# Four of six row transposes moved from TensorE to VectorE's 32 x 32 blocks and 32 small transfers per pass

## The chip, the cores and the metric

The kernel runs on one core of one Trainium2 chip. The metric is the device time of the whole kernel in microseconds; the median of three runs before the change is 877.59 us (877.58 to 877.67). The core has TensorE (matrix products, PE in the profile; its weight loads are PEld), VectorE (DVE), ScalarE (ACT), GpSimd (POOL) and SyncE (SP), each with its own queue of instructions in program order. They meet only through semaphores. Transfers are issued here by SyncE and, after the change, also by ScalarE.

## The reference

Three steps in a row, on 4 sequences of 448 positions with 768 channels (12 heads of 64):

```python
scores = scale * np.matmul(q, k.transpose(0, 1, 3, 2)) - np.log(S)
attn = 1.0 / (1.0 + np.exp(-scores)); x = attn @ v        # attention

xk = mu_k * x + (1 - mu_k) * x_prev; xr = mu_r * x + (1 - mu_r) * x_prev
k = np.maximum(xk @ w_k, 0.0); v = k * k @ w_v            # gated part
x = 1.0 / (1.0 + np.exp(-(xr @ w_r))) * v

h = np.maximum(x.transpose(0, 2, 1) @ w_tok1, 0.0) @ w_tok2   # along the positions
u = x + h.transpose(0, 2, 1)
out = u + np.maximum(u @ w_ch1, 0.0) @ w_ch2              # along the channels
```

The step that matters here is `x.transpose(0, 2, 1)`: the gated rows lie with channels on partitions, and the product with `w_tok1` needs them with positions on partitions.

## The kernel before

All work is done twice, for two sequences each time (`b0` is 0, then 2). The two sequences lie side by side, so that a tile is 128 channels by 2 x 448 = 896 columns, and 768 channels are six such tiles, m = 0 to 5. One pass is `attention`, `first_part`, `second_part`.

Every product is made with operands split into a high and a low part of a rounded format: three matmuls (high x high, high x low, low x high) stand for one. `products` writes them for one weight block: 896 columns are cut into 512 and 384, first all matmuls of one piece, then all of the other; the next call begins with the piece that the last one ended with.

Weights come as raw 64-bit numbers. For each block of weights there is a transfer (`w_raw`, SyncE), two ScalarE passes (`w_form`, L220 and L221), two VectorE passes (`w_join`, L224 and L227), a ScalarE copy to the rounded high part (`w_high`, L265, tile `whi`) and a VectorE subtraction for the low part (`w_low`, L269, tile `wlo`). `weights()` takes the next block and puts the steps for blocks further ahead in the list `due`; `products` runs one of them (`tick`) after every second slice of its loop. While block i is being multiplied, the queues get: high part of i+2; low part of i+2 and form of i+3; nothing; join of i+3 and the raw transfer of i+5. There are two raw buffers, two form buffers and three split buffers.

The stage that the change touches is the third loop of `first_part`: for m = 0 to 5, two weight blocks (`part` 0 and 1) of four slices each make 128 channels of `k*k @ w_v` in PSUM, and L416 multiplies them by the gate in `rows[:, m]`. Below, "the product of m" is that VectorE instruction. `hooks` maps a slice number to a function that is called after that slice in the second piece of a block: for m from 1 on, after slice 0 of part 0, `y_transpose(m - 1)`. It lets TensorE transpose the row tile m - 1 in eight pieces against an identity matrix (L352), and ScalarE and VectorE write high and low part from PSUM into `y` (L354 to L357; the last 64 positions have their low part in the upper 64 partitions).

Then come three pieces of the product with `w_tok1`, each on two row tiles (0 and 1, 2 and 3, 4 and 5), of 22 matmuls of 512 columns each. `y_transpose(NT - 1)` for tile 5 stands after piece 0, so that its eight transposes wait for the product of m = 5. The order of the work is that of the program; nothing is rearranged.

Buffers around the change: `xes`, six tiles with the attention output (two sequences of 1 + 448 columns; the first column is zeroed once at the start, L154), not in use in the stage; `kqs`, three tiles for queries and keys, not in use either; `two`, which holds `y` here.

Of the kernel before, what the change touches and what calls it, by code (L numbers as in the profile page):

```python
# [9 lines left out]
F32 = mybir.dt.float32  # L10
# [4 lines left out]
ALU = mybir.AluOpType  # L15
PSUM = bass.MemoryType.PSUM

B, H, S, D = 4, 12, 448, 64
# [4 lines left out]
P = 128  # L23
NT = C // P
NPAIR = H // 2
TAIL = S - 3 * P
W = 2 * S

WIDE = ((0, 512), (512, W - 512))
WARM = 9  # L30
KQ = 4 * P + S


def f32(ap):
    return ap.bitcast(F32)
# [3 lines left out]
def kernel(  # L39
# [17 lines left out]
    PE, ACT, DVE, POOL, SP = nc.tensor, nc.scalar, nc.vector, nc.gpsimd, nc.sync  # L57
# [4 lines left out]
    const = pool("const", 1)  # L62
# [12 lines left out]
    warm = const.tile([P, 1], F32, tag="warm", name="warm")  # L75
    ident = const.tile([P, P], F32, tag="ident", name="ident")
    mus = {n: [const.tile([P, NT], F32, tag=m + n, name=m + n) for m in ("mu", "om")] for n in "kr"}
    xes = [const.tile([P, 2, 1 + S], F32, tag="xe%d" % i, name="xe") for i in range(NT)]
    const.tile([P, 8], F32, tag="pad", name="pad")
    one = const.tile([P, 2 * NT * W], F32R, tag="one", name="one")  # L80
    two = const.tile([P, 2 * 4 * 2 * C], F32R, tag="two", name="two")
    three = const.tile([P, 4 * W], F32R, tag="three", name="three")
# [21 lines left out]
    def beside(ap):  # L104
        return ap.rearrange("p (b n) -> p b n", b=2)

    kqs = [const.tile([P, KQ], F32, tag="kq%d" % i, name="kq") for i in range(3)]
    vns = [const.tile([P, 7, D], F32, tag="vn%d" % i, name="vn") for i in range(4)]
    more = [const.tile([P, W], F32, tag="more%d" % i, name="more") for i in range(2)]
    kq_high = [two[:, 2 * i * KQ : (2 * i + 1) * KQ] for i in range(2)]  # L110
# [38 lines left out]
    for name, src in (("k", mu_k), ("r", mu_r)):  # L149
        m, om = mus[name]  # L150
        SP.dma_start(out=m, in_=src)
        DVE.tensor_scalar(out=om, in0=m, scalar1=-1.0, scalar2=1.0, op0=ALU.mult, op1=ALU.add)
    for t in xes:
        POOL.memset(t[:, :, 0:1], 0.0)  # L154

    places = [rows[:, m] for m in range(NT)] + more
    att = {}
# [162 lines left out]
    def products(ps, pieces, parts, at=0, count=None, hooks={}, in_turn=False):  # L320
        count = count or len(parts)
        runs = [pieces] if in_turn else [(p,) for p in pieces]
        if runs[-1][-1][1] == last[0]:
            runs.reverse()
        last[0] = runs[-1][-1][1]
        for r, run in enumerate(runs):
            for i, (wh, wl, xh, xl) in enumerate(parts, at):
                passes = [(wh, xh), (wh, xl), (wl, xh)] if xl is not None else [(wh, xh), (wl, xh)]
                for n, (w, x) in enumerate(passes):
                    for a, cols in run:  # L330
                        PE.matmul(  # L331
                            ps[:, a : a + cols],
                            w,
                            x[:, a : a + cols],
                            start=(i == 0 and n == 0),
                            stop=(i == count - 1 and n == len(passes) - 1),
                        )
                if in_turn or len(runs) == 1 or i % 2 or i == at + len(parts) - 1:
                    tick()
                if i in hooks and r == len(runs) - 1:  # L340
                    hooks[i]()
# [4 lines left out]
    def y_transpose(m):  # L346
        ps = new_ps()
        psv = ps.rearrange("p (r b c) -> p r b c", r=4, b=2)
        for r in range(4):
            n = P if r < 3 else TAIL  # L350
            for b in range(2):
                PE.transpose(psv[:n, r, b], rows[:, m, b * S + r * P : b * S + r * P + n], ident)  # L352
        hi, lo = (t[:, :, m] for t in y)
        ACT.copy(hi[:, :3], psv[:, :3])  # L354
        DVE.tensor_tensor(out=lo[:, :3], in0=psv[:, :3], in1=f32(hi[:, :3]), op=ALU.subtract)  # L355
        ACT.copy(hi[:TAIL, 3], psv[:TAIL, 3])
        DVE.tensor_tensor(out=hi[TAIL:, 3], in0=psv[:TAIL, 3], in1=f32(hi[:TAIL, 3]), op=ALU.subtract)  # L357

    def attention(b0):
        for t in range(NT):  # L360
            i, xe = b0 * NPAIR + 2 * t, xes[t]
            if t + 1 < NT:
                load_kq(i + 2)
            scores(i)
            if t + 1 < NT:
                load_kq(i + 3)
                load_v(i + 2)
                load_v(i + 3)
            if b0 == 0 and t == 0:
                w_raw(2)  # L370
            scores(i + 1)
            if t + 1 < NT:
                split_kq(i + 2)
                split_kq(i + 3)
            if b0 == 0 and 1 <= t < 5:
                w_form(t)
                w_join(t)
                w_raw(t + 2)
                w_high(min(t - 1, 3))
                w_low(min(t - 1, 3))  # L380
            ps = [values(i), values(i + 1)]
            value_tails(i, ps[0], xe)
            value_tails(i + 1, ps[1], xe)
            mix("r", t, xr, xe)

    def first_part(b0):
# [11 lines left out]
        for m in range(F // P):  # L398
# [7 lines left out]
            ACT.copy(hi, t)  # L406
            DVE.tensor_tensor(out=lo, in0=t, in1=f32(hi), op=ALU.subtract)

        for m in range(NT):
            ps = new_ps()  # L410
            for part in range(2):
                w = weights()
                parts = [(w[0][:, t], w[1][:, t], *kk(4 * part + t)) for t in range(4)]
                hooks = {0: lambda: y_transpose(m - 1)} if m and part == 0 else {}
                products(ps, WIDE, parts, 4 * part, 8, hooks)
            DVE.tensor_tensor(out=rows[:, m], in0=rows[:, m], in1=ps[:, :W], op=ALU.mult)  # L416

        wt1 = [weights()]
# [155 lines left out]
```

## Time and profile before

| What | Value |
|---|---|
| median of 3 runs | 877.59 us |
| the profiled execution | 878.26 us, its span 876.4 us |
| TensorE matmul busy | 871.5 us, 99% of the span |
| VectorE busy | 542.3 us, 62% |
| ScalarE busy | 416.3 us, 47% |
| chain of work that ended last | 98% TensorE |
| DMA engines, mean busy share | 33% |
| granted TensorE clock | 1.0 in all |

The span is the part of the execution that the profile shows; 1.9 us of the profiled execution lie around it. Busy shares are means over stages. Times in the rows are microseconds from the start of the span unless marked ns. A line such as L352 is a line of the kernel before.

### The profile page before, as it was taken

The page shows a single profiled execution, that of the slowest core. Times are in us where ns is not written, and L with a number is a line of the kernel's source. Part 1 is how long each engine was busy: PE and PEld are TensorE (multiplying, and loading weights), DVE is VectorE, ACT ScalarE, POOL GpSimd, SP SyncE. Part 2 cuts the span into 40 slices and gives each one's busy share as a digit, 9 for nine tenths or more (in the row PEclk, how much of TensorE's full clock was granted, in tenths as well). Part 3 has the DMA queues.
Part 4 walks back from the last instruction along what each step waited for, and adds up shares of the span by engine and source line. Part 5 has one row for each costly group of instructions (what it writes and reads, how often), then busy time and mean ns, then how long its engine had stood idle before and what let it go on. Part 6 is the DMA issues. An engine that isn't in the chain of part 4 may idle for free.

```text
span 876.4 us, 11347 instructions
## 1 busy us (share of the span) xinstructions
PE 871.5 (99%) x4637; PEld 735.2 (84%) x4637; DVE 542.3 (62%) x608; ACT 416.3 (47%) x550; POOL 1.3 (0%) x13
## 2 busy tenths in 40 slices
PE   9999999999999999999999999999999999999998
PEld 4557989899888989898955589899998898989897
DVE  3877976565676555555656498665566755555551
ACT  5894545444444433443366644555444444334420
POOL 0000000000000000000000000000000000000000
PEclk9999999999999999999999999999999999999999
DMA  7452323232322333334664023322234133333321
GB/s 268 142 172 87 124 86 101 86 97 96 132 73 73 109 109 108 108 108 153 235 234 133 22 75 109 105 84 74 95 101 164 37 109 108 109 108 108 109 99 63
DMA packets 29571, 98.90 MB, mean 113 GB/s; under 512 B 3536, under 2 KB 13008, under 8 KB 29520
## 3 DMA queue, kind: packets, MB, share of 16 engines
q1 hardware_dynamic: 29232, 97.73, 33.0%
q8 instruction: 36, 0.59, 0.3%
q10 hardware_dynamic: 288, 0.46, 0.1%
q14 instruction: 15, 0.12, 0.0%
HBM read 92.67 MB, written 5.51 MB: 112 GB/s over the span
## 4 chain that ended last, share of the span: by engine, by line
PE 98%; DVE 1%; DMA 1%; issue 0%; ACT 0%; POOL 0%; SPq 0%; ACTq 0%; POOLq 0%
PE ps L331 82%; PE ps L179 7%; PE ps L193 6%; PE ps L201 1%; PE ps L352 1%; DMA out_dram<-rows 1%; PE ps L141 0%; DVE two L161 0%; DVE rows L480 0%; DVE wd L227 0%; DVE wlo L269 0%; ACT rows L187 0%; DVE wd L224 0%; DVE rows L474 0%; POOL rows L138 0%
## 5 line engine op out<-in xcount | busy, mean ns | idle before, releaser
L331 PE MATMUL ps<-one,whi 128*128 128x512 f32 (+1 forms) x1152 | 323.7, 363 | 0.0
L331 PE MATMUL ps<-two,whi 128*128 128x512 f32 (+1 forms) x1044 | 295.8, 365 | 0.0
L331 PEld LDWEIGHTS ps<-one,whi 128*128 128x128 f32 x1152 | 211.5, 188 | 24.9 <-issue 1.4
L331 PEld LDWEIGHTS ps<-two,whi 128*128 128x128 f32 x1044 | 192.5, 188 | 23.2 <-DVE two L355 0.4
L331 PE MATMUL ps<-one,wlo 128*128 128x512 f32 (+1 forms) x576 | 207.3, 363 | 0.0
L331 PE MATMUL ps<-two,wlo 128*128 128x512 f32 (+1 forms) x528 | 191.1, 366 | 0.0
L265 ACT CAST whi<-wd 128x768 fp32r<-128x768 f32 (+1 forms) x104 | 80.8, 777 | 134.3 <-PE ps L331 91.8
L331 PEld LDWEIGHTS ps<-one,wlo 128*128 128x128 f32 x576 | 107.9, 188 | 11.4
L224 DVE SCALAR_TENSOR_TENSOR wd<-wd,raw 128x768 uint32<-128x768 uint32 (+1 forms) x104 | 92.2, 887 | 33.6 <-ACT raw L221 33.3
L331 PEld LDWEIGHTS ps<-two,wlo 128*128 128x128 f32 x528 | 98.9, 188 | 11.4
L269 DVE TENSOR_TENSOR wlo<-wd,whi 128x768 fp32r<-128x768 f32 (+1 forms) x104 | 91.6, 880 | 9.4 <-ACT whi L265 8.9
L227 DVE SCALAR_TENSOR_TENSOR wd<-raw,wd 128x768 uint32<-128x768 uint32 (+1 forms) x104 | 92.2, 887 | 3.6
L220 ACT ACTIVATE wd<-raw 128x768 f32<-128x768 f32 (+1 forms) x104 | 88.3, 849 | 3.5 <-DMA raw<-in_moe_w_ch_dram 3.5
L221 ACT ACTIVATE raw<-raw 128x768 uint32<-128x768 uint32 (+1 forms) x104 | 86.7, 833 | 0.0
L462 DVE SCALAR_TENSOR_TENSOR one<-ps,one 128x896 fp32r<-128x896 f32 x24 | 26.2, 1092 | 71.1 <-ACT one L461 71.1
L461 ACT ACTIVATE one<-ps 128x896 fp32r<-128x896 f32 x24 | 22.1, 921 | 95.8 <-PE ps L331 95.8
L480 DVE TENSOR_TENSOR rows<-rows,ps 128x896 f32<-128x896 f32 x23 | 25.0, 1088 | 67.4 <-PE ps L331 67.4
L187 ACT ACTIVATE rows<-ps 128x896 f32<-128x896 f32 x72 | 59.8, 938 | 11.5 <-PE ps L179 9.7
L179 PEld LDWEIGHTS ps<-two 64*128 64x128 f32 x528 | 47.8, 184 | 13.2 <-issue 7.4
L179 PE MATMUL ps<-two 64*128 64x448 f32 x528 | 57.7, 370 | 0.0
L193 PE MATMUL ps<-rows,vn 128*64 128x448 f32 x240 | 48.0, 545 | 0.1
L193 PEld LDWEIGHTS ps<-rows,vn 128*64 128x64 f32 x240 | 16.1, 136 | 26.8 <-issue 21.8
(69 smaller groups left out, 564.4 us busy)
## 6 DMA issues: line engine op xcount, KB each, us to landing
raw<-in_moe_w_ch_dram SPq DMA_DIRECT2D x48, 768.0 KB, 4.1
raw<-in_moe_w_k_dram SPq DMA_DIRECT2D x16, 768.0 KB, 4.2
raw<-in_moe_w_v_dram SPq DMA_DIRECT2D x24, 512.0 KB, 3.2
raw<-in_moe_w_r_dram SPq DMA_DIRECT2D x12, 768.0 KB, 4.2
kq<-in_k_dram SPq DMA_DIRECT2D x23, 256.0 KB, 4.5
vn<-in_v_dram SPq DMA_DIRECT2D x24, 224.0 KB, 4.5
kq<-in_q_dram SPq DMA_DIRECT2D x23, 224.0 KB, 4.8
out_dram<-rows SPq DMA_DIRECT2D x23, 224.0 KB, 2.1
```

Of the source, the lines that this page charges most:

```text
L179: PE.matmul(ps[:, h * 512 : h * 512 + S], x[me, at : at + P], y[me], start=(n == 0), stop=(n == len(passes) - 1),)
L187: ACT.activation(a, banks(ps), AF.Sigmoid, bias=-math.log(S), scale=1.0 / math.sqrt(D))
L193: PE.matmul(ps[h * D : h * D + D, :S], vns[i % 4][:, 3 * h + c], att[i % 2, c][:, h], start=(c == 0), stop=False)
L220: ACT.activation(f32(dst), f32(raw[..., 1]), AF.Copy, scale=2.0**-112)
L221: ACT.activation(raw[..., 0], raw[..., 0], AF.Copy, bias=0.4375, scale=0.875 * 2.0**-29)
L224: DVE.scalar_tensor_tensor(out=dst, in0=dst, scalar=3, in1=raw[..., 0], op0=ALU.logical_shift_left, op1=ALU.bitwise_or)
L227: DVE.scalar_tensor_tensor(out=dst, in0=raw[..., 1], scalar=0x80000000, in1=dst, op0=ALU.bitwise_and, op1=ALU.bitwise_or)
L265: ACT.copy(halves[i][0], forms[i])
L269: DVE.tensor_tensor(out=halves[i][1], in0=forms.pop(i), in1=f32(halves[i][0]), op=ALU.subtract)
L331: PE.matmul(ps[:, a : a + cols], w, x[:, a : a + cols], start=(i == 0 and n == 0), stop=(i == count - 1 and n == len(passes) - 1),)
L462: DVE.scalar_tensor_tensor(out=lo, in0=ps[:, :W], scalar=0.0, in1=f32(hi), op0=ALU.max, op1=ALU.subtract)
L480: DVE.tensor_tensor(out=rows[:, m], in0=rows[:, m], in1=ps[:, :W], op=ALU.add)
```

## The change

`y_transpose` stays for the row tiles 4 and 5. For the tiles 0 to 3 (`TURNED = 4`) three new functions replace it.

`y_turn(m)`: two VectorE instructions (one for each sequence) that transpose the tile within blocks of 32 x 32, into a buffer `turned`. There are two such buffers, one for tiles 0 and 1 in the memory of `xes`, one for tiles 2 and 3 in that of `kqs`, so both of these become one tile each that is cut up. A block transposed in place sits on the wrong partitions: `y_carry` moves the blocks to where they belong by 16 transfers for two tiles, issued by ScalarE, 32 in a pass. Each reads 32 partitions x 8 runs x 64 numbers (256 bytes a run, 64 KB in all) and writes 32 partitions of `staged`. `y_split(m)`: for each sequence two ScalarE copies and two VectorE subtractions, now from `staged` in SBUF, eight instructions in place of four.

`between(m, part)` sets the places, as hooks after the slices 0 to 3 of each block: `y_turn(m - 1)` where the transposes were; the transfers two at a time from the third slice of m = 2 and of m = 4 on; `y_split(0)` and `y_split(1)` in part 1 of m = 3, `y_split(2)` and `y_split(3)` in part 1 of m = 5. The zeroed columns of `xes`, which `staged` and `turned` overwrite, are zeroed at the start of each `attention`. One unused tile grows from 8 to 40 numbers.

```diff
+BLK = 32
+TURNED = 4
...
-    xes = [const.tile([P, 2, 1 + S], F32, tag="xe%d" % i, name="xe") for i in range(NT)]
-    const.tile([P, 8], F32, tag="pad", name="pad")
+    xes = const.tile([P, NT * 2 * (1 + S)], F32, tag="xe", name="xe")
+    const.tile([P, 40], F32, tag="pad", name="pad")
+    turned = xes[:, : 16 * P]
+    staged = xes[:, 16 * P : 32 * P].rearrange("p (s b r c) -> p s b r c", s=4, b=2, r=4)
...
-    kqs = [const.tile([P, KQ], F32, tag="kq%d" % i, name="kq") for i in range(3)]
+    kqs = const.tile([P, 3 * KQ], F32, tag="kq", name="kq")
+    turned = [t.rearrange("p (b g c) -> p b g c", b=2, c=2 * BLK) for t in (turned, kqs[:, : 16 * P])]
+    kqs = [kqs[:, i * KQ : (i + 1) * KQ] for i in range(3)]
...
+    def y_turn(m):
+        at = m % 2 * BLK
+        for b in range(2):
+            DVE.transpose(
+                turned[m // 2][:, b, : S // BLK, at : at + BLK],
+                rows[:, m, b * S : (b + 1) * S].rearrange("p (g c) -> p g c", c=BLK),
+            )
+
+    def y_carry(src):
+        def move(d, s):
+            ACT.dma_start(out=staged[d * BLK : (d + 1) * BLK, s], in_=src[s * BLK : (s + 1) * BLK, :, d::4])
+
+        return [lambda d=d, s=s: move(d, s) for d in range(4) for s in range(4)]
+
+    def y_split(m):
+        at = m % 2 * BLK
+        for b in range(2):
+            src = staged[:, :, b, :, at : at + BLK].rearrange("p s r c -> p r s c")
+            hi, lo = (t[:, :, m, b].rearrange("p r (s c) -> p r s c", c=BLK) for t in y)
+            ACT.copy(hi[:, :3], src[:, :3])
+            DVE.tensor_tensor(out=lo[:, :3], in0=src[:, :3], in1=f32(hi[:, :3]), op=ALU.subtract)
+            ACT.copy(hi[:TAIL, 3], src[:TAIL, 3])
+            DVE.tensor_tensor(out=hi[TAIL:, 3], in0=src[:TAIL, 3], in1=f32(hi[:TAIL, 3]), op=ALU.subtract)
...
+            def first():
+                if part == 0 and 0 < m <= TURNED:
+                    y_turn(m - 1)
+                elif part == 0 and m:
+                    y_transpose(m - 1)
+
+            def some():
+                for _ in range(2):
+                    if moves:
+                        moves.pop(0)()
+
+            def third():
+                if part == 0 and m in (2, 4):
+                    moves.extend(y_carry(turned[m // 2 - 1]))
+                some()
+
+            def second():
+                if part == 1 and m in (3, 5):
+                    y_split(m - 3)
+                some()
+
+            def fourth():
+                if part == 1 and m in (3, 5):
+                    assert not moves
+                    y_split(m - 2)
+                some()
+
+            return {at: first, at + 1: second, at + 2: third, at + 3: fourth}
...
-                hooks = {0: lambda: y_transpose(m - 1)} if m and part == 0 else {}
-                products(ps, WIDE, parts, 4 * part, 8, hooks)
+                products(ps, WIDE, parts, 4 * part, 8, between(m, part))
```

Two places in the order of instructions matter below. The first is VectorE's queue in m = 5 of the first pass. Before the change, from the low part of the second `w_tok1` block on (`wd` and `raw` are weight buffers, `rows` the gated tile, L416 the product of m = 5):

```order
L269 TENSOR_TENSOR wlo<-wd,whi 128x512
L224 SCALAR_TENSOR_TENSOR wd<-wd,raw 128x768
L227 SCALAR_TENSOR_TENSOR wd<-raw,wd 128x768
L416 TENSOR_TENSOR rows<-rows,ps 128x896
L269 TENSOR_TENSOR wlo<-wd,whi 128x768
```

The same stretch after the change (`xe` holds `staged`, `two` holds `y`; L387 and L389 are the subtractions of `y_split`, L483 is the product of m = 5):

```order
L276 TENSOR_TENSOR wlo<-wd,whi 128x512
L387 TENSOR_TENSOR two<-xe,two 128x3x128
L389 TENSOR_TENSOR two<-xe,two 64x128
L387 TENSOR_TENSOR two<-xe,two 128x3x128
L389 TENSOR_TENSOR two<-xe,two 64x128
L231 SCALAR_TENSOR_TENSOR wd<-wd,raw 128x768
L234 SCALAR_TENSOR_TENSOR wd<-raw,wd 128x768
L387 TENSOR_TENSOR two<-xe,two 128x3x128
L389 TENSOR_TENSOR two<-xe,two 64x128
L387 TENSOR_TENSOR two<-xe,two 128x3x128
L389 TENSOR_TENSOR two<-xe,two 64x128
L483 TENSOR_TENSOR rows<-rows,ps 128x896
```

Eight subtractions now stand ahead of the product of m = 5, four on either side of the join of a 768-column weight block.

The second is ScalarE's queue in the same m = 5. Before, from the copies of `y_transpose(4)` on:

```order
L354 CAST two<-ps 128x3x256
L356 CAST two<-ps 64x256
L265 CAST whi<-wd 128x512
L220 ACTIVATE wd<-raw 128x768
L221 ACTIVATE raw<-raw 128x768
L265 CAST whi<-wd 128x768
```

After (L361 and L363 are the copies of `y_transpose(4)`, L377 a transfer of `y_carry`, L386 and L388 the copies of `y_split(2)`):

```order
L361 CAST two<-ps 128x3x256
L363 CAST two<-ps 64x256
L377 DMA xe<-kq 32x8x64 x6
L272 CAST whi<-wd 128x512
L227 ACTIVATE wd<-raw 128x768
L228 ACTIVATE raw<-raw 128x768
L386 CAST two<-xe 128x3x128
L388 CAST two<-xe 64x128
L386 CAST two<-xe 128x3x128
L388 CAST two<-xe 64x128
```

The last six transfers stand between the copies of tile 4 and the next weight steps, and the first copy of `y_split(2)` follows these; the four copies of `y_split(3)` come behind.

## Rows read from the trace of the kernel before

**Rows 1.** The page: the span, and the chain that ended last by engine.

```profile
span 876.4 us, 11347 instructions
...
PE 98%; DVE 1%; DMA 1%; issue 0%; ACT 0%; POOL 0%; SPq 0%; ACTq 0%; POOLq 0%
```

**Rows 2.** Timeline of PE: start, us, engine, line, what, count.

```profile
172.86 0.62 PE L331 MATMUL ps<-one,whi 128*128 128x512 f32 x2
...
182.53 0.62 PE L331 MATMUL ps<-one,whi 128*128 128x512 f32 x2
...
185.77 1.03 PE L352 MATMUL ps<-ident,rows 128*128 128x128 f32 x8
...
193.05 0.62 PE L331 MATMUL ps<-one,whi 128*128 128x512 f32 x2
```

**Rows 3.** VectorE and ScalarE in the stage 176 to 237, by window.

```profile
core 0: us, PE busy (x) PEld busy (x) DVE busy (x) ACT busy (x) POOL busy (x), PEclk, DMA share, GB/s
176.00:237.00 61.00, 61.00 (x324) 55.14 (x323) 37.63 (x52) 27.26 (x47) 0.00 (x0) 1.00 0.31 104
```

**Rows 4.** Timeline of ACT in m = 5 and after (idle time before, releaser).

```profile
230.75 0.37 ACT L356 CAST two<-ps 64x256 fp32r<-64x256 f32 x1 [1.02 <-DVE two L355]
233.10 0.62 ACT L265 CAST whi<-wd 128x512 fp32r<-128x512 f32 x1 [1.99 <-DVE wd L227]
233.63 0.91 ACT L220 ACTIVATE wd<-raw 128x768 f32<-128x768 f32 x1
234.44 0.87 ACT L221 ACTIVATE raw<-raw 128x768 uint32<-128x768 uint32 x1
...
241.60 0.90 ACT L220 ACTIVATE wd<-raw 128x768 f32<-128x768 f32 x1 [1.76 <-DMA raw<-in_moe_w_ch_dram]
```

**Rows 5.** Timeline of DVE in m = 5 and after.

```profile
235.35 0.96 DVE L224 SCALAR_TENSOR_TENSOR wd<-wd,raw 128x768 uint32<-128x768 uint32 x1 [0.90 <-ACT raw L221]
236.34 0.96 DVE L227 SCALAR_TENSOR_TENSOR wd<-raw,wd 128x768 uint32<-128x768 uint32 x1
237.22 1.08 DVE L416 TENSOR_TENSOR rows<-rows,ps 128x896 f32<-128x896 f32 x1
...
245.20 0.95 DVE L355 TENSOR_TENSOR two<-ps,two 128x768 fp32r<-128x768 f32 x1
```

**Rows 6.** Timeline of PE from the stage's end on.

```profile
235.13 0.62 PE L331 MATMUL ps<-two,whi 128*128 128x512 f32 x2
...
240.12 1.03 PE L352 MATMUL ps<-ident,rows 128*128 128x128 f32 x8
...
246.03 0.68 PE L331 MATMUL ps<-two,whi 128*128 128x512 f32 x2
```

**Rows 7.** Groups by form, window 176 to 252: count, busy us, mean ns.

```profile
L269 DVE TENSOR_TENSOR wlo<-wd,whi 128x512 fp32r<-128x512 f32 x12 | 8.3, 688 | 4.4 <-ACT whi L265 4.4
...
L265 ACT CAST whi<-wd 128x512 fp32r<-128x512 f32 x12 | 7.4, 620 | 19.2 <-DVE wd L227 19.2
...
L357 DVE TENSOR_TENSOR two<-ps,two 64x256 fp32r<-64x256 f32 x6 | 2.5, 418 | 2.6 <-ACT two L356 2.6
...
L356 ACT CAST two<-ps 64x256 fp32r<-64x256 f32 x6 | 2.2, 366 | 7.3 <-DVE two L355 7.3
```

**Rows 8.** Issues by line: duration ns min/median/max, first and last start.

```profile
L475 ACTq DMA_DIRECT2D out_dram<-rows x1: 350/350/350, 873.5 to 873.5; - x1
...
L131 ACTq DMA_DIRECT2D kq<-in_q_dram x1: 409/409/409, 0.7 to 0.7; - x1
...
L251 SPq DMA_DIRECT2D raw<-in_moe_w_ch_dram x48: 327/328/328, 225.8 to 834.8; - x48
L251 SPq DMA_DIRECT2D raw<-in_moe_w_v_dram x24: 327/328/328, 144.3 to 645.3; - x24
```

**Rows 9.** The page's DMA issues: count, KB each, median us to landing.

```profile
kq<-in_q_dram SPq DMA_DIRECT2D x23, 224.0 KB, 4.8
out_dram<-rows SPq DMA_DIRECT2D x23, 224.0 KB, 2.1
```

More of the change, by code (lines that the diff above doesn't have):

```diff
@@ L77 @@
     mus = {n: [const.tile([P, NT], F32, tag=m + n, name=m + n) for m in ("mu", "om")] for n in "kr"}
-    xes = [const.tile([P, 2, 1 + S], F32, tag="xe%d" % i, name="xe") for i in range(NT)]
-    const.tile([P, 8], F32, tag="pad", name="pad")
+    xes = const.tile([P, NT * 2 * (1 + S)], F32, tag="xe", name="xe")
+    const.tile([P, 40], F32, tag="pad", name="pad")
+    turned = xes[:, : 16 * P]
+    staged = xes[:, 16 * P : 32 * P].rearrange("p (s b r c) -> p s b r c", s=4, b=2, r=4)
+    xes = [
+        xes[:, t * 2 * (1 + S) : (t + 1) * 2 * (1 + S)].rearrange("p (b n) -> p b n", b=2) for t in range(NT)
+    ]
     one = const.tile([P, 2 * NT * W], F32R, tag="one", name="one")
@@ L152 @@
         DVE.tensor_scalar(out=om, in0=m, scalar1=-1.0, scalar2=1.0, op0=ALU.mult, op1=ALU.add)
-    for t in xes:
-        POOL.memset(t[:, :, 0:1], 0.0)
     places = [rows[:, m] for m in range(NT)] + more
@@ L357, in y_transpose @@
         DVE.tensor_tensor(out=hi[TAIL:, 3], in0=psv[:TAIL, 3], in1=f32(hi[:TAIL, 3]), op=ALU.subtract)
+    def y_turn(m):
[18 more added lines that the diff above has]
+            DVE.tensor_tensor(out=hi[TAIL:, 3], in0=src[:TAIL, 3], in1=f32(hi[:TAIL, 3]), op=ALU.subtract)
     def attention(b0):
+        for xe in xes:
+            POOL.memset(xe[:, :, 0:1], 0.0)
         for t in range(NT):
@@ L407, in first_part, with between @@
             DVE.tensor_tensor(out=lo, in0=t, in1=f32(hi), op=ALU.subtract)
+        moves = []
+        def between(m, part):
+            at = 4 * part
+            def first():
[21 more added lines that the diff above has]
+            return {at: first, at + 1: second, at + 2: third, at + 3: fourth}
         for m in range(NT):
```

## The prediction

> **What bounds the kernel now.** I read the chain of work that ended last first: 98% of the span of 876.4 us is TensorE [rows 1], so a change counts by what it takes from TensorE's queue and by what it makes that queue wait. Then the timeline of TensorE in the stage of the change: one row tile without transposes takes 182.53 - 172.86 = 9.67 us, the next one, with eight transposes that start at 185.77, takes 193.05 - 182.53 = 10.52 us, with no pause in it [rows 2]. Then the windows of the other engines: in the 61 us of the stage VectorE works 37.6 and ScalarE 27.3 [rows 3], so both have room on the whole. Last the place where the stage hands over, in the timelines of the three engines: the product of m = 5 runs on VectorE from 237.22 to 238.30 [rows 5], and TensorE asks for it at 240.12, when the transposes of tile 5 come up [rows 6]. There are 1.8 us of room, and in this stretch both queues get longer.
>
> **The change part by part.**
>
> What goes. Four of the six groups of transposes in each of two passes. A group costs 10.52 - 9.67 = 0.85 us of TensorE's time [rows 2]; 8 x 0.85 = 6.8 us. All of it lies on the chain. The skill weighs the same step otherwise: the Trainium skill, VectorE: DVE Perf Modes, "The three transpose paths", gives 390 ns for one 128 x 128 transpose on TensorE against 311 ns on VectorE (bf16, blocks only). By it the 64 transposes would be 25 us and the result near 857 us; the row of this case shows eight in 0.85 us, because they follow one another without a pause, and I go by the row.
>
> What VectorE gets. Two block transposes for a tile of 448 columns each in place of the two subtractions of 0.95 and 0.42 us [rows 5, 7]. No row shows a block transpose. By the subtractions of 512 and 256 columns, 0.69 and 0.42 us [rows 7], 448 columns are 0.62 us, so 1.24 us for a tile against 1.37 before. At half of that or at twice of that it stays within the 23 us that VectorE has free in the stage [rows 3], and TensorE no longer waits for it; I take nothing. In m = 3 and m = 5 come eight subtractions: 384 columns at 0.55 and 128 at 0.28 us by the same two rows, 0.83 for one sequence, 1.66 for a tile, 3.3 for both.
>
> What ScalarE gets. 32 issues in a pass. Its own two issues took 0.35 and 0.41 us, those of SyncE 0.33, whether 512 or 768 KB [rows 8]. I take 0.38, 12 us in a pass. Those all moved one row per partition; the new ones have eight runs on each of 32 partitions, 256 in place of 128. The bounds are 0.33 and, were the time to go by the number of runs, 0.66 us. The copies of `y_split` are 0.49 and 0.25 us by the rows of 512 and 256 columns [rows 7]. With 34 us free in the stage [rows 3] this fits on the whole; the order decides.
>
> What it does in m = 3 of a pass. From the start of m = 3 (0), part 1 begins at 4.84. ScalarE then makes a high part and a form of 512 columns (0.5 and, two thirds of what 768 columns take below, 1.2 us), the first copy ends at 7.1, VectorE's first four subtractions at 8.8, a join (two thirds of 1.95) at 10.1, the other four at 11.8, the product of m = 3 at 12.8, the next low part at 13.5. TensorE wants that low part when part 1 of m = 4 begins, at 14.5. Nothing on TensorE waits for the product of m = 3 itself, since its tile is turned by VectorE. So 1 us of room, no cost.
>
> What it does in m = 5, in the clock of the profile of before. TensorE keeps the transposes of tile 4, so the copies of that tile end as before, at 230.75 + 0.37 = 231.1 [rows 4]. Behind them on ScalarE now stand six issues: 6 x 0.38 = 2.3, 233.4. Then the high part (233.10 to 233.63, 0.5 us) and the form of a 768-column block (233.63 to 235.31, 1.7 us) [rows 4]: 235.6. The first copy of `y_split(2)`: 236.1. Its transfers have landed by then: the last issue starts at 233.0, and rows leaving for DRAM take 2.1 us to land [rows 9]. VectorE is the slower one from here: four subtractions, 1.66, 237.8; the join of the 768-column block, 235.35 to 237.30, 1.95 us [rows 5], 239.7; four subtractions, 241.4; only then the product of m = 5, 1.08 us [rows 5], 242.5. Before, the join and the product stood ahead of nothing else and were done at 238.3. TensorE's piece 0 still ends at 240.12 [rows 6], so TensorE waits 2.4 us for tile 5, in each of two passes: 4.7 us.
>
> What is late next. The raw transfer for the block after next starts when that join is done; its form came 241.60 - 237.30 = 4.3 us after it [rows 4, 5], and the subtraction for tile 5 7.9 us after it, at 245.20. With the join at 239.7 that subtraction runs from 247.6 to 248.55. TensorE, 2.4 us later than before, begins piece 2 at 246.03 + 2.4 = 248.4 [rows 6] and needs the low part one matmul later. That is as tight as before (246.15 against 246.03); nothing added.
>
> The sum. -6.8 + 4.7 = -2.1 us. The profiled execution of 878.26 would be 876.2 and its span 874.3. The median of the runs lies 0.67 us under the profiled execution; 877.59 - 2.1 = 875.5 us.
>
> **The rivals.**
>
> All of it hidden, 877.6 - 6.8 = 870.8 us. For it: both engines have room in the window, and issues may overlap with the copy before them on ScalarE. Against it: even with issues that cost nothing the high part waits for a join until 233.10 [rows 4], the first copy ends near 235.8, and the same steps give 242.2. Only copies and subtractions at half of what the rows give would do it.
>
> Issues at twice the time, slower, about 881 us. The mechanism: an issue takes ScalarE as long as the runs of the transfer are many, 0.66 us for 256 runs. The six in m = 5 then end 1.7 us later. And m = 4 no longer clears its queue: four issues from 14.5 on (the block transpose of tile 3), a high part and a form, six issues, and again a high part and a form end at 24.6 after the start of m = 3, while the transposes of tile 4 are done at 23.4; 1.2 us more. TensorE waits 2.4 + 2.9 = 5.3 us in each pass, -6.8 + 10.6 = +3.8 us. The point from which it costs more than it brings is a wait of 3.4 us, an issue of 0.55 us. For it: no issue of before has more than 128 runs [rows 8]. Against it: 512 and 768 KB cost the same 0.33 us. The Trainium skill, Perfetto Trace Analysis, "DMA Instruction — HWDGE", says that the issuing queue is held until all descriptors of the transfer are generated; no run here shows what their number costs.
>
> Transfers that land late, 880 us. Loads of queries take 4.8 us to land [rows 9]. If a move from SBUF to SBUF takes that, the last one lands at 237.8 and not 235.1; the first copy is 2.2 us later, the wait 4.6 us, -6.8 + 9.2 = +2.4 us. For it: 256 short runs. Against it: rows that leave SBUF land in 2.1 us with 3.5 times the bytes.
>
> **How the numbers follow.** What a measurement of this kernel can tell from no change is about 0.2%, 1.75 us: under 875.83 is faster, over 879.35 slower. Forecast 0.55, in itself from 874 to 877.5 us, as the issue takes 0.33 to 0.5 us and as the short instructions come out a little shorter or longer; its middle is close to the line, 0.30 faster and 0.25 the same. All hidden 0.10, faster. Issues at twice the time 0.23, of which 0.20 slower. Late landing 0.12, of which 0.08 slower. Together faster 0.40, the same 0.32, slower 0.28. The range that holds 8 of 10 cuts a part of the first rival and what is beyond the second: 872.0 to 881.5 us.
>
> **What would show it.** Right, if row tiles m = 1 to 4 take 9.7 us on TensorE; if after piece 0 TensorE stands still for 2 to 3 us in each pass and the releaser named is VectorE's product of m = 5; if that product starts about 4 us later than before against TensorE's own clock, behind the last subtraction of `y_split(3)`; if ScalarE's issues are 0.33 to 0.41 us. Wrong, if TensorE goes through from piece 0 to the transposes; if an issue is over 0.5 us; if the first copy of `y_split(2)` waits for a transfer; or if TensorE stops inside m = 3 or m = 4 for a weight block.

## The result, and the profile after

The changed kernel takes 890.2 us (median of 5 runs, 888.32 to 891.18) against 877.67 us for the kernel before on the same chip. The ratio is 1.0132, 95% interval [1.0115, 1.015]: 12.5 us slower, where 2.1 us faster was forecast and the range ended at 881.5. The profiled execution took 888.32 us, its span is 886.6 us against 876.4 [rows 1].

The chain that ended last had been TensorE's to 98% [rows 1]. In the page of the kernel after, the other engines, the transfers and their issues have come in (shares of the span):

```profile
span 886.6 us, 11409 instructions
...
PE 86%; DVE 5%; DMA 4%; ACT 2%; ACTq 1%; issue 1%; POOL 0%; SPq 0%; POOLq 0%
```

What TensorE waited for, in total, how often, and the longest one (L359 are the transposes, L483 is the product of m):

```profile
PE ps L359 <- DVE rows L483: 13.5, 2, 7.4
```

The timeline of TensorE answers to [rows 6]: piece 0 ends, the transposes of tile 5 come up, and the first matmul of piece 2, behind the 22 of piece 1, follows after the "...". The number in brackets is the idle time ahead of the instruction and what ended it. The second pass shows the same with 6.12 us.

```profile
236.02 0.39 PE L338 MATMUL ps<-two,wlo 128*128 128x512 f32 x1
243.79 1.97 PE L359 MATMUL ps<-ident,rows 128*128 128x128 f32 x8 [7.39 <-DVE rows L483]
...
251.74 0.61 PE L338 MATMUL ps<-two,whi 128*128 128x512 f32 x2
...
682.04 1.97 PE L359 MATMUL ps<-ident,rows 128*128 128x128 f32 x8 [6.12 <-DVE rows L483]
```

The place is the one forecast, the product of m = 5 ahead of the transposes of tile 5, and the wait is three times as long. It also has a second price: eight transposes take 1.97 us in place of 1.03. In the windows that follow, the clock granted to TensorE (the column PEclk, as a share of 2.4 GHz) is 0.60 and 0.74, means over its two levels: it had gone to 1.2 GHz while TensorE stood still, and was back at 2.4 GHz only some us after TensorE worked again.

```profile
core 0: us, PE busy (x) PEld busy (x) DVE busy (x) ACT busy (x) POOL busy (x), PEclk, DMA share, GB/s
194.00:236.00 42.00, 42.00 (x212) 37.64 (x211) 24.81 (x40) 16.23 (x31) 0.19 (x2) 1.00 0.55 150
236.00:240.00 4.00, 0.41 (x2) 0.00 (x0) 2.67 (x6) 2.55 (x8) 0.00 (x0) 1.00 0.00 0
240.00:246.00 6.00, 2.21 (x10) 2.04 (x11) 5.84 (x9) 2.73 (x4) 0.33 (x4) 0.60 0.38 132
246.00:250.00 4.00, 4.00 (x15) 3.21 (x14) 2.98 (x4) 2.09 (x3) 0.00 (x0) 0.74 0.48 184
250.00:254.00 4.00, 4.00 (x19) 3.31 (x18) 2.91 (x4) 2.32 (x3) 0.00 (x0) 1.00 0.60 209
```

From the start of the transposes to the first matmul of piece 2 it is 251.74 - 243.79 = 7.95 us, against 246.03 - 240.12 = 5.91 before [rows 6]: 2.0 us for the slow clock. In the second pass the same stretch takes 7.32 us, 1.4 more. The account: -6.8 for the eight groups that are gone, +7.4 + 6.1 waits, +2.0 + 1.4 slow clock: +10.1 us, and the spans differ by 886.6 - 876.4 = 10.2.

Why the product is late stands in the timeline of ScalarE, which answers to [rows 4]:

```profile
226.51 0.78 ACT L361 CAST two<-ps 128x768 fp32r<-128x768 f32 x1
228.31 0.36 ACT L363 CAST two<-ps 64x256 fp32r<-64x256 f32 x1 [1.02 <-DVE two L362]
228.32 3.90 ACTq L377 DMA_DIRECT2D xe<-kq  x6
232.32 0.62 ACT L272 CAST whi<-wd 128x512 fp32r<-128x512 f32 x1 [3.64 <-DMA xe<-kq]
232.85 0.91 ACT L227 ACTIVATE wd<-raw 128x768 f32<-128x768 f32 x1
233.65 0.89 ACT L228 ACTIVATE raw<-raw 128x768 uint32<-128x768 uint32 x1
236.62 0.51 ACT L386 CAST two<-xe 128x384 fp32r<-128x384 f32 x1 [2.08 <-DMA xe<-kq]
```

Six issues hold ScalarE for 3.90 us, and behind the form it waits another 2.08 us until the last of these transfers has landed. VectorE then goes through its queue in the order shown ahead of the prediction: subtractions from 237.16, the join from 238.98, subtractions from 240.84, and the product last (answers to [rows 5]):

```profile
242.65 1.09 DVE L483 TENSOR_TENSOR rows<-rows,ps 128x896 f32<-128x896 f32 x1
```

The issues by line (duration in ns, min/median/max, first and last start) and the time from issue to landing:

```profile
L377 ACTq DMA_DIRECT2D xe<-xe x32: 592/622/722, 194.8 to 645.0; - x32
L377 ACTq DMA_DIRECT2D xe<-kq x32: 592/622/1398, 216.6 to 670.0; - x32
...
DMA to landing us min/median/max: 2.1/3.3/5.2
```

0.62 us against the 0.33 to 0.41 of [rows 8]. With the gap between two it is 3.90 / 6 = 0.65 us, and 32 of them are 21 us. In the window 194 to 236 ScalarE is busy for 16.2 us besides. That is 37 of 42 us at most, in a queue that also has to wait for VectorE's joins; some issues run beside ScalarE's own work (the one of 1.40 us, the longest in the list, starts at 219.38, and L227, a pass of the form, at 219.77), and with the overlap counted once 31.8 us are taken.

Which transfers land late can be read from the times. In the middle of the six issues SyncE issues a load of raw weights; the four transfers ahead of it (window 228.3 to 230.5) and the two behind it (230.92 to 232.2) land differently (KB each, median us from issue to landing):

```profile
230.66 0.33 SPq L258 DMA_DIRECT2D raw<-in_moe_w_ch_dram  x1
...
xe<-kq ACTq DMA_DIRECT2D x4, 64.0 KB, 2.1
...
raw<-in_moe_w_ch_dram SPq DMA_DIRECT2D x1, 768.0 KB, 5.1
xe<-kq ACTq DMA_DIRECT2D x2, 64.0 KB, 5.0
```

The load lands at 235.79, the two transfers behind it at 236.12 and 236.44. Of the 64 transfers of this execution, 38 were issued while such a load was under way; each landed behind it, 2.6 to 5.2 us after its own issue. Of the other 26, 24 needed 2.1 to 2.7 us, and during the issue of the remaining two a load was issued. No run moves the loads, so this is read from the times and not tested.

### The profile page after: what moved, and what is told of

The parts are those of the page before. It is cut to its first block, busy times and chain, and to the rows that moved or that the text cites. A ratio compares the mean times of both kernels' runs of the same rounds, so it can differ in the third digit from the quotient of the medians.

```text
span 886.6 us, 11409 instructions
## 1 busy us (share of the span) xinstructions
PE 867.8 (98%) x4573; PEld 731.1 (82%) x4573; DVE 553.1 (62%) x640; ACT 417.3 (47%) x566; POOL 1.8 (0%) x19
## 3 DMA queue, kind: packets, MB, share of 16 engines
q10 hardware_dynamic: 17696, 4.66, 2.4%
## 4 chain that ended last, share of the span: by engine, by line
PE 86%; DVE 5%; DMA 4%; ACT 2%; ACTq 1%; issue 1%; POOL 0%; SPq 0%; POOLq 0%
PE ps L338 71%; PE ps L186 7%; PE ps L200 6%; PE ps L208 1%; ACTq L377 1%; DMA xe<-kq 1%; DMA raw<-in_moe_w_tok_dram 1%; DMA xe<-xe 1%; DMA raw<-in_moe_w_v_dram 1%; DVE wd L234 1%; DVE wd L231 1%; DVE rows L483 1%; DVE two L387 1%; DMA out_dram<-rows 1%; DVE two L389 1%
## 5 line engine op out<-in xcount | busy, mean ns | idle before, releaser
L227 ACT ACTIVATE wd<-raw 128x768 f32<-128x768 f32 (+1 forms) x104 | 88.4, 850 | 4.3 <-DMA raw<-in_moe_w_ch_dram 4.3
```

Of the source, the lines that this page charges most:

```text
L227: ACT.activation(f32(dst), f32(raw[..., 1]), AF.Copy, scale=2.0**-112)
```

## The experiments

The theory to test, A: the transfers' issues on ScalarE, and their landing, make the splits late, and with them the product that stands behind. The rivals, named in the expectations: the cost is the number of packets or the transfers wherever they are issued (B, C, D), the order alone, or the form of the weights.

**The product first.** The two calls of `y_split` in m = 5 are made after the loop over m, behind the product of m = 5:

```
-                if part == 1 and m in (3, 5):
+                if part == 1 and m == 3:
...
+        for m in (2, 3):
+            y_split(m)
         wt1 = [weights()]
```

> One edit: y_split(2) and y_split(3) are called after the third loop, so that on VectorE the product of m = 5 no longer stands behind their eight subtractions; the 32 transfers on ScalarE stay as they are. Theory A (order and late data together make the wait): the product is then bound by the join behind the six issues, near 237.5 in the clock of the changed kernel, TensorE waits 1 to 1.5 us for tile 5 and then 2 to 2.5 us at the second piece, which needs tiles 2 and 3, near 240.8: about 4 us per pass in place of 7.5 and 6.3, less of the low clock; 878 to 882 us. Theory B (only the late transfers count; wherever the product stands, TensorE has to wait for tiles 2 and 3): the wait moves to the second piece and keeps its size, 885 us or more.

882.2 us, ratio 1.0053 [1.0032, 1.0073]: 8 us of the loss are gone, 11 us above the 870.8 of "all hidden" stay. The time is 0.2 us above theory A's range and 3 below theory B's. TensorE now waits in many places for a little each:

```profile
PE ps L338 <- DVE two L387: 2.8, 2, 1.4
PE ps L359 <- DVE rows L483: 1.5, 1, 1.5
...
PE ps L338 <- ACT whi L272: 0.8, 1, 0.8
PE ps L338 <- DVE two L362: 0.6, 1, 0.6
```

With 0.4 for copies that is 6.1 us. The clock fell here too, behind waits of 1.5, 0.2 and 1.4 us within 5 us (PEclk 0.57 in 242 to 246). The chain goes through the six issues and a landing of 4.71 us as before. So the order was part of the loss, and the issues are another.

**SyncE issues them.** Four at a place instead of two:

```
-            ACT.dma_start(out=staged[d * BLK : (d + 1) * BLK, s], ...
+            SP.dma_start(out=staged[d * BLK : (d + 1) * BLK, s], ...
```

> One edit: SyncE issues the 32 transfers, four at a hook instead of two (16 are out before m = 5); the order on VectorE and ScalarE is otherwise that of the changed kernel, the product of m = 5 still behind the subtractions. Theory A (0.62 us an issue on ScalarE, and the last six issued and landed late): the copies of tile 4 start when its transposes end, no copy waits for a transfer, the product ends near 237.8, TensorE waits about 1.6 us per pass without a fall of the clock; 874 to 877 us. Theory C (the transfers are slow whichever queue issues them, or hold up the raw weights on SyncE): copies still wait for transfers, or ScalarE's forms for raw weights; 882 us or more.

892.3 us, ratio 1.0159 [1.0144, 1.0174]. An issue takes SyncE 0.61 us too (median). Now the raw weights, which SyncE brings, come late, and the chain leads from them over the form to the splits:

```profile
231.91 4.95 DMA raw<-in_moe_w_ch_dram
...
238.62 0.40 ACT two L386
...
244.54 1.10 DVE rows L483
```

This is theory C: the queue that was relieved is not the one that decided alone, since the same work ahead of the raw transfers ends in the same product.

**Fewer packets.** In the first pass half the bytes, 32 x 4 runs of 256 bytes; in the second 32 runs of 2 KB.

> The same 64 transfers on ScalarE in the same places, but with fewer runs: in the first pass 32 partitions x 4 runs of 256 bytes (only the first sequence is moved, 128 runs), in the second pass 32 partitions x 1 run of 2 KB (32 runs, the bytes of the changed kernel, but not the blocks that belong there). The output is not the reference's. Theory A (the issue time goes by the number of runs): 0.33 to 0.45 us in the first pass and 0.33 or less in the second against 0.62, landing near 2 us; waits of 2 to 3 us per pass, 875 to 879 us. Theory D (the time is that of a transfer of 32 partitions, or of SBUF to SBUF, or of ScalarE's turn beside its own work, not of the runs): 0.6 us in both passes, landing above 3 us, 885 us or more.

885.8 us, ratio 1.0087 [1.0072, 1.0102]. The packets of ScalarE's queue fall from 17,696 to 6,432. The issue does not get shorter; the second pass of it:

```profile
L381 ACTq DMA_DIRECT2D xe<-xe x16: 514/602/612, 632.7 to 643.0; - x16
```

So the theory that an issue takes long because its runs are many, the condition of the prediction's second rival, is wrong, though its price is right. The transfers still land after up to 5.7 us in the first pass and 5.2 in the second. Theory D has the time and the issue; which of its three reasons holds is tested below.

**Two rows instead of four.** `TURNED = 2`, 16 transfers a pass in m = 2 and 3, both splits in m = 3.

> TURNED = 2: tiles 0 and 1 are turned by VectorE with 16 transfers per pass in m = 2 and 3 and split in m = 3; tiles 2 to 5 keep their transposes on TensorE. Theory A (all the loss is in m = 5): four groups less, 4 x 0.85 = 3.4 us, no new wait, the product of m = 5 at its old place; 874.2 us, 873.5 to 875. Theory E (issues on ScalarE and subtractions in m = 3 delay the next weights): TensorE waits in m = 3 or 4; 877 us or more.

892.8 us, ratio 1.0164 [1.0148, 1.0179]: theory A, as it stood, fell here. Half of the issues, and the loss is no smaller, since tile 3 is now turned by TensorE and its product stands behind the eight subtractions, which are late:

```profile
PE ps L359 <- DVE rows L483: 12.2, 2, 6.3
```

The wait has moved from tile 5 to tile 3, 6.3 and 5.9 us, with the clock down behind it again (0.60 in 220 to 224). For a wait of this length it takes both: subtractions ahead of a product that a transpose waits for, and issues ahead of the subtractions (without any issue, below, the wait is 2.1 us).

**Two rows, and the splits behind the product of m = 3.** Row 0's split in m = 4, row 1's in m = 5:

```
-                if part == 1 and m in (3, 5):
-                    y_split(m - 3)
+                if part == 1 and m in (4, 5):
+                    y_split(m - 4)
...
-                if part == 1 and m in (3, 5):
-                    assert not moves
-                    y_split(m - 2)
```

> Two rows turned by VectorE instead of four, and the sixteen subtractions' place changed: the parts of row 0 are made in m = 4 and those of row 1 in m = 5, both behind the product of m = 3. Theory A (what cost the time is only that a product which TensorE's next transposes wait for stood behind splits that were late through ScalarE's issues, and the clock then fell): no wait is left, four groups of transposes are gone, 877.6 - 3.4 = 874.2 us, between 873.0 and 875.5. Rival B (sixteen issues of 0.62 us, 10 us a pass on ScalarE, delay the weights' forms wherever they stand): 877.6 or more, with TensorE waiting for whi or for a form in m = 3 or 4.

883.2 us, ratio 1.0056 [1.0044, 1.0069]. Rival B is right on the time. The long waits are gone and short ones came at four transposes (3.0 us) and in piece 0 (2.9). The chain of waits, in order of time, for the first of them:

```profile
209.85 2.06 DMA xe<-xe
...
212.42 0.66 ACT wd L227
...
213.68 0.70 DVE wd L231
...
215.10 1.01 DVE rows L480
...
216.15 1.11 PE ps L359 x8
```

Six issues, a form, the joins, the product (L480 here), the transposes: the form of the weights is a second way from an issue to a product. The waits, 5.9 us, less the 3.4 us gained, make 2.5; the span is 5.1 us longer than before. The other 2.6 us the list of waits does not show.

**GpSimd issues them**, with the product of m = 5 first (`POOL.dma_start`).

> As the run with the product of m = 5 first (882.2), with the 32 transfers of a pass issued by GpSimd, which has nothing else to do in this stage. Theory A (ScalarE's lost time, 32 x 0.62 = 20 us a pass, is what still cost 11 us there): the forms and copies come in time again, 871 to 875 us. Rival D (the transfers come late whoever issues them, because of their landing, or because GpSimd needs longer than 0.62 us for one): 880 or more, with TensorE or VectorE waiting for the last transfer.

901.1 us, ratio 1.0259 [1.0244, 1.0275], the slowest. One issue is 0.58 us on GpSimd too, but pauses of 0.5 to 3.1 us lie between, and the last starts at 243.76, when piece 1 should run. TensorE waits up to 6.1 us for a copy of the split. Rival D, by the pauses and not by the issue.

**Half of the transfers, in the order of the change.**

```
-        return [lambda d=d, s=s: move(d, s) for d in range(4) for s in range(4)]
+        return [lambda d=d, s=s: move(d, s) for d in range(2) for s in range(4)]
```

> The changed kernel with 16 of the 32 transfers of a pass (the lower half of the four rows' partitions alone is moved, the rest of the computation goes on with what stood there before, so the output is not the reference's); order of splits and products as in the changed kernel. Theory A (number of issues times 0.62 us on ScalarE makes the splits late): ScalarE is clear of transfers 5 us earlier in m = 4 and 5, the product of m = 5 is in time or nearly, 871 to 874 us. Rival B (the order alone, eight subtractions ahead of the product, is enough): TensorE still waits 4 us or more for the product of m = 5 in each pass and the clock falls, 879 or more.

877.0 us, ratio 0.9986 [0.9976, 0.9995]. The half that is left out costs 13 us, and the half that stays next to nothing (with none at all, below, the time is the same). Left out are, among others, the six issues that stood between the copies of tile 4 and the splits in m = 5. Neither theory has it whole. What stays, in a profiled execution that is the slowest of ten (880.1 us):

```profile
PE ps L359 <- DVE rows L483: 4.6, 2, 2.5
```

**Four forms of transfer.** In place of the 16 of one `y_carry`: L378 128 partitions of 512 bytes to the same partitions, L380 32 partitions of 1 KB to the same ones, L382 32 partitions of 1 KB from device memory, L387 32 partitions of 1 KB to other ones.

> A measurement of the issue alone, its time of no interest: four forms of transfer in the place of the 16 of a sequence, four of each (the output is not the reference's): 128 partitions of 512 B from on-chip memory to the same partitions; 32 partitions of 1 KB to the same partitions; 32 partitions of 1 KB from device memory; 32 partitions of 1 KB to other partitions, as in the change. The run with fewer packets had left the issue at 0.60 to 0.61 us. Theory F (from on-chip memory to on-chip memory is what costs): 0.6 us for the first, second and fourth, 0.35 to 0.41 for the third, as for the loads of before. Theory G (32 partitions instead of 128 cost): 0.35 to 0.41 for the first alone. Theory H (each issue that follows another at once takes 0.6): all four 0.6.

```profile
L378 ACTq DMA_DIRECT2D xe<-xe x8: 535/612/624, 194.3 to 631.6; - x8
...
L380 ACTq DMA_DIRECT2D xe<-xe x8: 568/606/612, 197.1 to 634.3; - x8
...
L382 ACTq DMA_DIRECT2D xe<-in_k_dram x16: 317/434/807, 199.6 to 662.7; - x16
...
L387 ACTq DMA_DIRECT2D xe<-xe x8: 514/572/602, 202.4 to 639.8; - x8
```

Theory F: from on-chip memory to on-chip memory an issue is 0.57 to 0.62 us (medians, those with `kq` as source included), whether for 32 or 128 partitions, the same or others; from device memory 0.43, a little above the 0.35 to 0.41 expected.

**One transfer at a place**, two rows turned, the product of m = 3 first (the loop in `some` runs once). The last two transfers come behind row 0's split, so row 0's parts are not the reference's.

> The run with two turned rows and the product of m = 3 ahead of the splits (883.2 us), with one transfer at a place in the program instead of two, so that ScalarE never issues more than about three in a row between two forms of the weights. Its chain of waits had led from the last six issues of m = 2 (3.9 us) to a form and the joins, and from there to the product. Theory A (blocks of issues ahead of a form are what is late): TensorE's waits of 6 us go, 873.5 to 876.5 us. Rival E (any sixteen issues are too much for the chain of form, join, product and transposes, since its lateness is handed on from one m to the next): 878 or more, with the product of m = 2, 3 or 4 late again.

881.7 us, ratio 1.0043 [1.003, 1.0055]: 1.6 us better than two at a place, and rival E's time. No product is late in m = 2 and 3 any more; that of m = 4 is, by 1.0 us in each pass. Between its form and its joins stands row 0's split.

**The same with SyncE** as the issuer (and the same two late transfers).

> The same as the run with one transfer at a place, with SyncE issuing them. Theory A (ScalarE's time alone matters): no issue stands ahead of a form, 873.5 to 875.5 us. Rival C (the raw weights' transfers stand behind the moves and behind their wait for VectorE's turn on SyncE, and are as late as the issues made the forms): 877 or more, with a form waiting for raw weights in m = 2 to 4.

886.7 us, ratio 1.0102 [1.0086, 1.0117]. Slower by SyncE a second time; the product of m = 4 is late by 3.4 us. Rival C has the time, but the order of things is the other way round: the moves come late because they stand behind the raw weights. Ahead of row 0's first copy ScalarE stands still for 2.2 us in the first pass, where the trace names no releaser, and for 2.3 in the second, where it names a transfer of this kind. In the first pass SyncE issued a load of raw weights at 220.92 and a move at 221.30; the load landed at 224.47, the move at 224.72, and the copy starts at 224.86.

**No transfers.** The change with its turns, splits and order, and `range(0)` in place of `range(4)`.

> The changed kernel without its transfers: VectorE's sixteen turns, the splits and the order of all else as in the change, but nothing is put in place (the output is not the reference's, the splits read what stood there). Theory A (the transfers' issues and their landing are the whole loss; half of them gave 877.0): 870.5 to 872.5 us, TensorE waits nowhere. Rival B (the sixteen subtractions and copies ahead of the products cost something by themselves): TensorE still waits 1 us or more for the product of m = 5 in each pass, 873.5 or more.

877.0 us, ratio 0.9989 [0.998, 0.9998]. Rival B: the order alone costs something, 2.1 us of wait in each pass:

```profile
PE ps L359 <- DVE rows L483: 4.2, 2, 2.1
```

VectorE's queue in the first pass of this run, from the first subtraction to the product, where the first copy of the split, and with it the first subtraction, comes behind the form as in the forecast:

```profile
230.97 0.56 DVE L387 TENSOR_TENSOR two<-xe,two 128x384 fp32r<-128x384 f32 x1 [1.28 <-ACT two L386]
...
232.79 0.96 DVE L231 SCALAR_TENSOR_TENSOR wd<-wd,raw 128x768 uint32<-128x768 uint32 x1
...
236.46 1.09 DVE L483 TENSOR_TENSOR rows<-rows,ps 128x896 f32<-128x896 f32 x1
```

-6.8 + 4.2 = -2.6 us, and the span of this execution is 2.9 us below before. In its other runs the mean granted clock is mostly 0.998 instead of 1.000, and their median is 1.1 us below before.

**Half of the transfers and the product first.** The edits of the first run and of the one with half of the transfers together.

> The changed kernel with half of its transfers (16 of 32 a pass, so the output is not the reference's) and with the splits of rows 2 and 3 behind the product of m = 5: both remedies at once. Half the transfers alone and no transfers at all gave the same 877.0, each with TensorE waiting 2.1 to 2.5 us a pass for the product. Theory K (two separate costs: the eight subtractions ahead of the product, 2 x 2.1 us and the clock behind them, and the issues that go beyond ScalarE's spare time in the stage, which half of them do not): both are gone, 870.5 to 872.5 us. Rival L (the subtractions put behind the product make piece 1 or piece 0 wait by as much): 874.5 or more, with TensorE waiting for a subtraction.

874.8 us, ratio 0.9963 [0.9949, 0.9977]. TensorE no longer waits at a transpose, but 1.3 us for tile 5's parts and 0.8 for subtractions of the splits, in two passes. By the time and by these waits it is rival L, though the waits are half of those with the product last. -6.8 + 2.1 = -4.7 us, and the span of this execution is 3.6 us below before. The difference lies behind the last matmul: the last transfer of the output lands 3.0 us after its issue, against 1.9 before. Why is open.

**The splits in the gaps.** Two rows; ten transfers in m = 2 and six in m = 3; `y_split` in two parts, its copies right behind those of the transposes and its subtractions behind the join that follows:

```
-                for _ in range(2):
+                for _ in range(2 if m == 2 else 1):
...
+                if part == 0 and m in (4, 5):
+                    assert not moves
+                    y_split(m - 4, False)
...
+                if part == 0 and m in (4, 5):
+                    y_split(m - 4, True)
```

The first of the two calls is in `second` and makes the copies, the other is in `fourth` and makes the subtractions.

> Two rows turned instead of four (16 transfers a pass, ten of them in m = 2 and six in m = 3, one or two at a place), row 0's copies and subtractions in m = 4 and row 1's in m = 5, each in the gaps that ScalarE and VectorE had there: the copies ahead of the next weights' high part, where ScalarE waited 2.0 us for the joins, the subtractions behind those joins. Theory K (with the issues within ScalarE's spare time and the splits in gaps nothing is late): 877.9 - 3.4 = 874.5 us, between 873.5 and 876. Rival E (any split ahead of a product that transposes wait for makes it late, since form, join, split, product and transposes are one chain through both engines): TensorE waits 0.5 us or more at the transposes of tile 4, 877 or more.

875.1 us (873.87 to 875.81, 5 runs), ratio 0.9964 [0.995, 0.9977]: 3.1 us faster than before, 15 us faster than the change, and nothing is left out of the computation. TensorE does not wait in the stage at all; the longest pieces of its chain are its own work again (start, us, what):

```profile
214.83 0.87 PE ps L359 x8
215.70 9.65 PE ps L338 x48
225.35 0.87 PE ps L359 x8
```

ScalarE and VectorE in m = 4, where the first row's split is now:

```profile
218.87 0.29 ACT L388 CAST two<-xe 64x128 fp32r<-64x128 f32 x1
219.92 0.62 ACT L272 CAST whi<-wd 128x512 fp32r<-128x512 f32 x1 [0.76 <-DVE wd L234]
```

```profile
219.75 0.55 DVE L390 TENSOR_TENSOR two<-xe,two 128x384 fp32r<-128x384 f32 x1
...
223.50 1.08 DVE L485 TENSOR_TENSOR rows<-rows,ps 128x896 f32<-128x896 f32 x1
```

The copies lie in time in which ScalarE waited for the join, 2.0 us, of which 0.76 are left. The product of m = 4 starts at 223.50 and the transposes want it at 225.35. The issues are as long as in the change (0.62 us), 16 of them: 10 us a pass. Against the two earlier runs with two rows, this one has other places for the issues, the copies and the subtractions at once; which of the three counts most is not taken apart.

## Why the prediction was wrong

What was right: the eight groups of transposes are worth 0.85 us each, since the run with four fewer of them and no wait is 3.1 us faster (3.4 forecast). The block transposes (0.62 us each, 0.602 to 0.641) and the splits' copies and subtractions (0.51, 0.29, 0.56, 0.28) are what the nearest rows gave. The place was right too, VectorE's product of m = 5, in both passes, and so was the cost of the order: the sentence that issues at no cost give a product at 242.2, 2.1 us behind 240.12, is what the run without transfers measured, 2.1 us a pass. The prediction used it against the rival of all hidden; it says as well that eight subtractions ahead of a product that TensorE waits for are a cost by themselves.

The step that failed is "What it does in m = 5", in three terms and one that was left out. The wait was put at 2.4 us; it was 7.4 in the first pass. Counted back from the end of piece 0, 236.4:

- The copies of tile 4 ended 7.7 us ahead of it (at 228.7), not 240.12 - 231.1 = 9.0: 1.3 us of backlog from m = 4. The forecast had a cleared queue there; only the rival with long issues had one that is not.
- The six issues end at 232.2, 3.5 us behind those copies, not 2.3: 1.2 us. The term is the issue at 0.38 us; it was 0.62, and 0.65 with the gap. The rival took 0.66, for another reason: neither the number of runs nor that of partitions is what takes the time, it is a transfer within on-chip memory.
- The first copy of the split starts at 236.6 and not behind the form, at 234.5: 2.1 us, by a landing of 4.84 us in place of 2.1. This is the late landing of the third rival, which had 2.2 us for it.

1.3 + 1.2 + 2.1 = 4.6 of the 5.0 us; in the second pass the same three are 0.2, 1.2 and 1.9 of 3.7. Put otherwise, two rivals held together that were priced apart: 5.3 us of wait with long issues and 2.2 for the landing are 7.5. Each had a chance of its own; both at once had none, and the range ended short of the sum. Both were among the prediction's signs of being wrong: an issue over 0.5 us, and a first copy of `y_split(2)` that waits for a transfer.

The third rival's reason, that a move within on-chip memory lands as slowly as a load, is not what the times show: a move took 2.1 us, and more where a load of weights stood ahead of it. The late landing may thus come from the long issues. At 0.38 us and the same gap, six issues from 228.32 on would all have started by 230.4, ahead of the load at 230.66; in the second pass by 668.8, ahead of the load at 669.04. This is an estimate from these rows; no run tests it.

The term left out is the clock: 2.0 + 1.4 us behind waits of 7.4 and 6.1 us. Without it the kernel would be 3.4 us better.

The loss thus has two parts. By order, with no transfers or half of them, the change gains 1.1 to 1.3 us where 6.8 were to be had. By transfers, the other half adds 13 us in the places that the change gives them. Their number alone does not explain this: in the three earlier runs with two turned rows and ScalarE as the issuer, 16 transfers a pass came with 14.6, 5.0 and 3.5 us more than before, and in the last run with less than before. The prediction's sum "34 us free in the stage" and "this fits on the whole" held, with 37 of 42 us at most; what did not fit is the stretch from the copies of tile 4 to the product of m = 5.

On the issue, the Trainium skill, Perfetto Trace Analysis, "DMA Instruction — HWDGE (DVE, Sync)", says that a queue is held until the descriptors are made. The trace agrees in that ScalarE starts nothing between 228.32 and 232.32, while the six are issued. A price by the number of runs, which the prediction's rival rested on, no run shows: 32 runs of 2 KB took 0.60 us, 256 of 256 bytes 0.62.

## What to carry to other kernels

An issue holds the queue of the engine that issues it: price it by a row of the same source and destination, and where there is none, count the issues times the largest bound against the spare time of that engine in the very stretch, and not in the stage. Before anything is put into an in-order queue, look for the next instruction in it that the bounding engine waits for; what fits without cost is what lies in a gap in which that queue waits for another engine, as the splits did in the last run. When one rival can bring another with it, as a longer issue can put a transfer behind a load, give their sum a chance and a place in the range, and add to a wait of several us the time that the clock takes to come back.

## What the runs showed of the hardware

A transfer from on-chip memory to on-chip memory took 0.57 to 0.62 us to issue (medians) on ScalarE, 0.61 on SyncE and 0.58 on GpSimd, against 0.33 to 0.43 for those with device memory at one end. Between 32 and 256 runs, and between 32 and 128 partitions, the medians differed by no more than 0.05 us.

In the changed kernel a transfer of 64 KB within on-chip memory landed 2.1 to 2.7 us after its issue (24 of the 26 that were issued while no load of weights was under way), and 2.6 to 5.2 us after it, always behind the load, where a load of 512 or 768 KB was (38).

TensorE's granted clock was 1.2 GHz behind waits of 6.1 and 7.4 us. It also fell behind waits of 2.5 and 2.1 us in the run with half of the transfers (0.80 in 238 to 242, 0.59 in 674 to 678), and behind two waits of 2.1 us in the profiled run without transfers it stayed at 2.4 GHz. In the run with the product first it fell behind waits of 1.5, 0.2 and 1.4 us (0.57 in 242 to 246). So the length of the wait alone does not say whether it falls.

Block transposes of 448 columns in fp32 took VectorE 0.62 us, as long as the prediction's estimate for a subtraction of that size from its neighbours' rows.
